# Linear attention before a mixture of experts: a product moved to GpSimd, and a scan's operand, small loads, bias and padding moved with it

## The chip, the cores and the metric

The kernel runs on one core of one Trainium2 chip. The metric is the device time of one execution in microseconds, as a median of repeated runs. The engines are named as the profile names them: PE (TensorE), DVE (VectorE), ACT (ScalarE), POOL (GpSimd) and SP, whose queue here only issues DMAs.

## What is computed

Three layers follow one another. The first is attention with a decaying state, for 4 batches, 8 heads, 768 tokens and heads of 48; the second sends each of the 3072 tokens through one of 8 experts, which a gate with a bias per modality chooses; the third is a dense layer with a squared relu.

```python
def _attn_ref(q, k, v, alpha):
    state = np.zeros((B, H, D, D), dtype=np.float32)
    for t in range(S):
        state = alpha[:, :, t, :, None] * state + np.einsum('bhd,bhe->bhde', k[:, :, t], v[:, :, t])
        y[:, :, t] = np.einsum('bhd,bhde->bhe', q[:, :, t], state)

def _moe_ref(x, modality_id, w_gate, modality_bias, w1, w2):
    logits = x @ w_gate + modality_bias[modality_id]
    e_idx = np.argmax(logits, axis=1)
    ...
    for e in range(E):
        mask = e_idx == e
        h = np.maximum(x[mask] @ w1[e], 0.0)
        out[mask] = gate_w[mask, None] * (h @ w2[e])

def _moe2_ref(x, w_in, w_out):
    r = np.maximum(x @ w_in, 0.0)
    return ((r * r) @ w_out).astype(np.float32)
```

## The kernel before

**Attention by chunks.** The 3072 tokens are 24 chunks of 128, six to a batch. In a chunk the decays are turned into running products, so that attention becomes matmuls. Queries, keys and decays of a chunk lie in one tile `qk` of 112 partitions: two heads side by side on rows 0 to 47 and 64 to 111, four pairs along the columns, with rows 48 to 63 as padding. For chunk n, `prep(n)` on DVE makes `acum`, the forward scan of the decays (line 472), its reciprocal at the chunk's end (473), `rs`, the backward scan (477), `qt`, the queries times `acum` (481), and `kt`, the keys times `rs` (483). A scan takes two operands, and the second here is `amin`, one constant column, spread over the row. It stands in column 384 of `kvc`, a PSUM bank, whose columns 0 to 383 PE writes with the products of keys and values. Engines do not touch one PSUM bank's tile at the same time in this kernel's trace: its `kvc` matmuls follow the scans, and the scans the matmuls.

**A round.** The loop runs over n from 0 to 23. PE does in order: `sp`, keys by queries of chunk n+1 (`qk_mm`, line 504); `kp`, the transpose of its `kt` (515); `kvc`, keys by values of chunk n (529); `y` of chunk n (554) and, from the second chunk of a batch on, its cross part with the state (557). ACT copies `sp` to `pm` (507), `kp` to `kT` (517) and `y` to `yt` (559). POOL masks `pm` of chunk n+1 (`affine_select`, 493; tied by hand to begin after the last operation of DVE that stands ahead of it) and multiplies the state by its decay (544). DVE does `prep(n+3)`, with two hooks: `kv_sd`, which adds the state (541, 543), between the two scans, and the jobs called "D", behind the backward scan. The code's order is the order of every engine's queue; nothing is reordered by a scheduler. A new `sp` needs `qt` and `kt`; a new `kvc` needs `kT` only, though the bank holds it for the scans as well.

**The gate.** Every fourth round `gate_lg` multiplies `yt` by the gate's weights into the bank `gps` (218); ACT copies it to `ls`, and `back` transposes it (226) into the same bank. In rounds 8 and 16 (eight chunks at a time) `gate_a` follows as a "D" job on DVE: `L`, `mx`, `dl` (238), `sc`, `sm`, `oh_all` (243). In the next round PE counts with `gate_b` (250, 252) from `oh_all`; DVE's `gate_s` makes the weights `gw` through `ss` (282 to 285) and `gate_c` the ranks. With `gw` ACT scales each chunk's transposed output (`xtr`, 293) to `xb` (297). From `bt_all`, `first_ids` picks, again into `gps`, the tokens of the first expert, which POOL gathers (633) near the end of the loop.

**The start.** SP's queue loads chunks 0 to 3 and three tiles of values, then the gate's weights `wg`, the modalities `mod`, the biases `mbias`, and writes zeros to a table `pbuf` in DRAM (194), then loads chunk 4 and so on. DMAs share eight counts in turn, so that each DMA waits for the one that last used its count; in the order's rows these counts are DMAHW0 to DMAHW7. `mask(0)` stands behind `qk_mm(0)`; the bias table `lbias` is made by five operations of DVE in round 2 (`setup_bias`).

**Behind attention** come the experts (three matmuls for one product in split precision) and the dense layer, whose conversions of weights run on POOL (lines 733 and 734).

Of the kernel before, what the change touches and what calls it, by code (L numbers as in the profile page):

```python
# [57 lines left out]
def body(ctx, tc, qka, v, alpha, mod, wg, mbias, w1, w2, w_in, w_out, out):  # L58
# [123 lines left out]
    def setup_gate():  # L182
# [11 lines left out]
        SY.dma_start(pbuf.rearrange("(o n) -> o n", n=C), sdt[2][:(NT + PAD) // C, :C].bitcast(I32))  # L194

    def setup_bias():
        modf = gc.tile([128, NTILE, 1], F32, name="modf")
        V.tensor_copy(modf, mod_sb[:, :, 0:1])
        modn = gc.tile([128, NTILE, 1], F32, name="modn")
        V.tensor_scalar(modn, modf, -1.0, 1.0, op0=ALU.mult, op1=ALU.add)  # L200
        lb1 = gc.tile([128, NTILE, NE], F32, name="lb1")
# [1119 lines left out]
```

## Time and profile before

| what | value |
|---|---|
| median of 3 runs | 776.43 us (776.18 to 777.32) |
| the profiled execution | 774.81 us, its span 773.0 us |
| granted PE clock, mean | 0.995 |
| busy share of the span | PE 96%, DVE 62%, ACT 42%, POOL 21% |

The page's busy shares are means over three layers of different kind. Attention lasts to about 124 us; experts and dense layer follow. To read a stretch, one takes the timeline of one engine at a time, finds two equal operations a round apart, and looks at the brackets, which give the idle time before an instruction and what ended it.

### The profile page before, as it was taken

The page shows a single profiled execution, that of the slowest core. Times are in us where ns is not written, and L with a number is a line of the kernel's source. Part 1 is how long each engine was busy: PE and PEld are TensorE (multiplying, and loading weights), DVE is VectorE, ACT ScalarE, POOL GpSimd, SP SyncE. Part 2 cuts the span into 40 slices and gives each one's busy share as a digit, 9 for nine tenths or more (in the row PEclk, how much of TensorE's full clock was granted, in tenths as well). Part 3 has the DMA queues.
Part 4 walks back from the last instruction along what each step waited for, and adds up shares of the span by engine and source line. Part 5 has one row for each costly group of instructions (what it writes and reads, how often), then busy time and mean ns, then how long its engine had stood idle before and what let it go on. Part 6 is the DMA issues. An engine that isn't in the chain of part 4 may idle for free.

```text
span 773.0 us, 13143 instructions
## 1 busy us (share of the span) xinstructions
PE 745.1 (96%) x5148; PEld 654.0 (85%) x5148; DVE 478.0 (62%) x812; ACT 323.8 (42%) x587; POOL 166.2 (21%) x185
## 2 busy tenths in 40 slices
PE   8898989999999999999999999999999999999994
PEld 6777778898788888889889989999899998999984
DVE  7999997877887867878744444544553333343340
ACT  3446467354444443546533323332332342333340
POOL 3332323234645454431100100010020001002001
PEclk9999999999999999999999999999999999999998
DMA  8988765579877886788300220040010000001001
GB/s 216 266 210 237 208 212 164 167 199 221 158 278 221 214 221 157 251 159 230 126 5 1 66 85 0 11 140 1 0 42 2 1 10 31 1 1 42 0 1 45
DMA packets 42814, 88.89 MB, mean 115 GB/s; under 512 B 11181, under 2 KB 26567, under 8 KB 42743
## 3 DMA queue, kind: packets, MB, share of 16 engines
q1 hardware_dynamic: 39543, 78.13, 36.1%
q0 software_dynamic: 3200, 9.83, 4.6%
q8 instruction: 42, 0.69, 0.4%
q14 instruction: 29, 0.24, 0.1%
HBM read 72.19 MB, written 15.76 MB: 114 GB/s over the span
## 4 chain that ended last, share of the span: by engine, by line
PE 76%; DVE 5%; DMA 2%; ACT 1%; issue 1%; POOL 0%; POOLq 0%; DVEq 0%; ACTq 0%
PE acc L660 8%; PE acc L658 8%; PE acc L659 8%; PE h L659 8%; PE h L660 8%; PE h L658 8%; PE hps L659 4%; PE hps L660 4%; PE oo L658 4%; PE oo L659 4%; PE oo L660 4%; PE hps L658 4%; DMA xg<-xs,ids 1%; DVE w2l L569 1%; PE xt L651 1%
## 5 line engine op out<-in xcount | busy, mean ns | idle before, releaser
L1044 DVE TENSOR_TENSOR r<-r 128x512 f32<-128x512 f32 x96 | 68.7, 716 | 143.8 <-ACT r L1043 143.7
L660 PE MATMUL acc<-w2h,hl 128*128 128x384 f32 x372 | 125.7, 338 | 0.3 <-DVE hl L569 0.2
L658 PE MATMUL acc<-w2h,hh 128*128 128x384 f32 x372 | 125.3, 337 | 0.6 <-ACT hh L568 0.6
L659 PE MATMUL acc<-w2l,hh 128*128 128x384 f32 x372 | 124.9, 336 | 0.0
L1043 ACT ACTIVATE r<-h 128x512 f32<-128x512 f32 x96 | 57.4, 598 | 154.4 <-PE h L660 153.0
L660 PE MATMUL h<-xh,w1l 128*128 128x512 f32 x288 | 113.8, 395 | 0.0
L659 PE MATMUL h<-xl,w1h 128*128 128x512 f32 x288 | 113.6, 395 | 0.0
L658 PE MATMUL h<-xh,w1h 128*128 128x512 f32 x288 | 112.1, 389 | 0.0
L569 DVE TENSOR_TENSOR hl<-r,hh 128x512 fp32r<-128x512 f32 x93 | 64.5, 694 | 63.9 <-PE acc L660 36.4
L1067 POOL DMA_INDIRECT out_dram<-ob,pidx x24 | 23.9, 995 | 366.4 <-ACT ob L1065 328.8
L568 ACT CAST hh<-r 128x512 fp32r<-128x512 f32 x93 | 57.7, 620 | 80.6 <-DVE r L1044 80.6
L658 PEld LDWEIGHTS acc<-w2h,hh 128*128 128x128 f32 x372 | 69.9, 188 | 5.1 <-ACT hh L568 1.0
L659 PEld LDWEIGHTS acc<-w2l,hh 128*128 128x128 f32 x372 | 69.8, 188 | 3.8
L660 PEld LDWEIGHTS acc<-w2h,hl 128*128 128x128 f32 x372 | 69.8, 188 | 1.0 <-DVE hl L569 1.0
L658 PE MATMUL oo<-hh,w2h 128*128 128x512 f32 (+1 forms) x192 | 68.7, 358 | 0.0
L658 PE MATMUL hps<-xh,w1h 128*128 128x512 f32 (+1 forms) x192 | 68.1, 355 | 0.0
L659 PE MATMUL hps<-xl,w1h 128*128 128x512 f32 (+1 forms) x192 | 67.4, 351 | 0.7 <-DVE xl L569 0.7
L660 PE MATMUL oo<-hh,w2l 128*128 128x512 f32 (+1 forms) x192 | 67.3, 350 | 0.0
L659 PE MATMUL oo<-hl,w2h 128*128 128x512 f32 (+1 forms) x192 | 67.2, 350 | 0.0
L660 PE MATMUL hps<-xh,w1l 128*128 128x512 f32 (+1 forms) x192 | 67.1, 350 | 0.0
L660 PEld LDWEIGHTS h<-xh,w1l 128*128 128x128 f32 x288 | 54.0, 188 | 11.5
L659 PEld LDWEIGHTS h<-xl,w1h 128*128 128x128 f32 x288 | 54.0, 187 | 9.2
(217 smaller groups left out, 1281.0 us busy)
## 6 DMA issues: line engine op xcount, KB each, us to landing
qk<-qka_dram SPq DMA_DIRECT2D x21, 679.0 KB, 5.7
raw<-w_dram SPq DMA_DIRECT2D x21, 512.0 KB, 8.1
raw<-w_dram SPq DMA_DIRECT2D x28, 384.0 KB, 4.2
cvr<-w_in_dram SPq DMA_DIRECT2D x12, 512.0 KB, 5.9
cvr<-w_out_dram SPq DMA_DIRECT2D x12, 512.0 KB, 11.6
vv<-v_dram SPq DMA_DIRECT2D x24, 192.0 KB, 6.7
xs<-xb SPq DMA_DIRECT2D x24, 192.0 KB, 3.5
alr<-alpha_dram SPq DMA_DIRECT2D x9, 512.0 KB, 3.4
```

Of the source, the lines that this page charges most:

```text
L568: A.copy(hi, raw)
L569: V.tensor_sub(lo, raw, hi)
L651: PE.transpose(xt[:, hf * 128:(hf + 1) * 128], xgs[i][:, hf, k * 128:(k + 1) * 128], ident)
L658: PE.matmul(o, ah, bh, start=start, stop=False)
L659: PE.matmul(o, ah, bl, start=False, stop=False)
L660: PE.matmul(o, al, bh, start=False, stop=stop)
L1043: A.activation(r, o, AF.Relu)
L1044: V.tensor_mul(r, r, r)
L1067: G.indirect_dma_start(out=out, out_offset=bass.IndirectOffsetOnAxis(ap=pidx[:, n:n + 1], axis=0), in_=ob, in_offset=None)
```

## The change

`kt` is made by POOL from chunk 2 on, in `prep` right behind the backward scan. `qt` is made ahead of the backward scan, between `kv_sd` and it, and the state's decay, still on POOL, is called behind `qt` and tied to begin after it. The "D" jobs stand behind `kt`. `amin` goes from `kvc` to column 511 of `gps`; the logits of `gate_lg` go from `gps` to a part of the current `y` tile. The four `qk` tiles are allocated once, and from chunk 4 on a chunk is loaded by two DMAs of 48 rows, without the padding rows. The loads of `wg`, `mod` and `mbias` and the write of `pbuf` go from SP's queue to ACT's. `setup_bias` is done by POOL, at the start behind `mask(0)`, and `mask(0)` stands behind `prep(1)`, tied to its last operation.

```diff
+        if n < 4:
+            qks.append(ld.tile([RP, 2 * NP * C + NP * CA], F32, name=f"qk{n}", bufs=1))
+        qk = qks[n % 4]
...
         else:
-            SY.dma_start(qk, qka[b, c])
+            for j in range(2):
+                SY.dma_start(qk[64 * j:64 * j + D], qka[b, c, 64 * j:64 * j + D])
...
-    amin = kvc[:, 2 * NP * D:2 * NP * D + 1]
+    gps = ps_g.tile([128, 512], F32, name="gps")
+    amin = gps[:RP, 511:512]
...
-        SY.dma_start(wg_sb[64 * j:64 * j + D, :, :NE], wg.rearrange("(p j d) e -> j d p e", j=2, d=D)[j])
+        A.dma_start(wg_sb[64 * j:64 * j + D, :, :NE], wg.rearrange("(p j d) e -> j d p e", j=2, d=D)[j])
...
-        SY.dma_start(pbuf.rearrange("(o n) -> o n", n=C), sdt[2][:(NT + PAD) // C, :C].bitcast(I32))
+        A.dma_start(pbuf.rearrange("(o n) -> o n", n=C), sdt[2][:(NT + PAD) // C, :C].bitcast(I32))
...
-        lt = gps[:, :128]
+        lt = gps[:, :128] if n_y[0] is None else n_y[0][:, 0, 2 * C:3 * C]
...
+        qt = xp.tile([RP, NP, C], F32, tag="xl", name="qt", bufs=4)
+        if n > 1:
+            V.tensor_mul(qt, qq, acum[:, :, 1:C + 1])
+        for f in mids[1:2]:
+            f(last_dve())
         rs = at2.tile([RP, NP, CA], F32, tag="rs", name="rs", bufs=1)
         V.tensor_tensor_scan(rs.rearrange("p a c -> p (a c)")[:, ::-1], al[:, ::-1], amin, AMIN, op0=ALU.mult, op1=ALU.max)
-        for f in mids[1:]:
+        kt = xp.tile([RP, NP, C], F32, tag="xh", name="kt", bufs=4)
+        if n < 2:
+            V.tensor_mul(qt, qq, acum[:, :, 1:C + 1])
+        (V if n < 2 else G).tensor_tensor(kt, kk, rs[:, :, 2:C + 2], op=ALU.mult)
+        for f in mids[2:]:
             f()
-        qt = xp.tile([RP, NP, C], F32, tag="xl", name="qt", bufs=4)
-        V.tensor_mul(qt, qq, acum[:, :, 1:C + 1])
-        kt = xp.tile([RP, NP, C], F32, tag="xh", name="kt", bufs=4)
-        V.tensor_tensor(kt, kk, rs[:, :, 2:C + 2], op=ALU.mult)
...
-    mask(0)
     k_T(0)
     warm(FILL)
     preps[1] = prep(1)
+    mask(0, last_dve())
+    setup_bias()
...
-    at(2, "mid", setup_bias)
...
-            preps[n + 3] = prep(n + 3, lambda: kv_sd(n), lambda: do(n, "D"))
+            preps[n + 3] = prep(n + 3, lambda: kv_sd(n), lambda i: decay(n, i), lambda: do(n, "D"))
```

In the order of ACT at its start, before, the conversions of six small tables are followed by the first copy of `pm`. The names in brackets are counts that an instruction waits for: PE_49 is PE's, Pool_49 POOL's, DMAHWn_49 a DMA's.

```order
L160 CAST tokid<-tokid_i 128x24 [waits Pool_49]
L160 CAST hidx<-hidx_i 128x22 [waits Pool_49]
L160 CAST slj<-slj_i 128x6 [waits Pool_49]
L160 CAST edesc<-edesc_i 128x8 [waits Pool_49]
L160 CAST eidx<-eidx_i 128x8 [waits Pool_49]
L507 COPY pm<-sp 128x512 [waits PE_49] x2
L517 COPY kT<-kp 128x448 [waits PE_49]
```

The same place now, with the DMAs that came from SP's queue:

```order
L151 DMA wg_sb<-wg_dram 48x4x8 [waits DMAHW0_49,Pool_49]
L151 DMA wg_sb<-wg_dram 48x4x8 [waits DMAHW1_49]
L153 DMA mod_sb<-mod_dram 128x48 [waits DMAHW2_49]
L155 DMA mb_sb<-mbias_dram 128x16 [waits DMAHW4_49]
L165 CAST rev<-rev_i 128x128 [waits Pool_49]
L165 CAST tokid<-tokid_i 128x24 [waits Pool_49]
L165 CAST hidx<-hidx_i 128x22 [waits Pool_49]
L165 CAST slj<-slj_i 128x6 [waits Pool_49]
L165 CAST edesc<-edesc_i 128x8 [waits Pool_49]
L165 CAST eidx<-eidx_i 128x8 [waits Pool_49]
L199 DMA pbuf<-sd_128 26x128 [waits DMAHW7_49]
L521 COPY pm<-sp 128x512 [waits PE_49] x2
```

The write of `pbuf` stands ahead of the first copy and waits for DMAHW7; the last DMA in SP's queue on that count at this point is the load of chunk 3.

In the order of DVE in round 8, with the gate's jobs ("D") of the first eight chunks, before:

```order
L472 SCALAR_TENSOR_TENSOR acum<-qk,kvc 112x528 [waits DMAHW4_49,PE_49]
L473 RECIPROCAL qk<-acum 112x4 [waits DVE_49]
L543 TENSOR_TENSOR sd_127<-kvc,sd_126 112x192 [waits Pool_49]
L477 SCALAR_TENSOR_TENSOR rs<-qk,kvc 112x528 [waits DVE_49]
L234 TENSOR_TENSOR L<-gps,lbias 128x64 [waits PE_49]
L236 TENSOR_REDUCE mx<-L 128x8 [waits DVE_49]
L238 TENSOR_TENSOR dl<-L,mx 128x64 [waits DVE_49]
L240 SCALAR_TENSOR_TENSOR sc<-dl,edesc 128x64 [waits DVE_49]
L242 TENSOR_REDUCE sm<-sc 128x8 [waits DVE_49]
L243 TENSOR_TENSOR oh_all<-sc,sm 128x64 [waits DVE_49]
L481 TENSOR_TENSOR qt<-qk,acum 112x512
L483 TENSOR_TENSOR kt<-qk,rs 112x512
```

The same round now:

```order
L478 SCALAR_TENSOR_TENSOR acum<-qk_110,gps 112x528 [waits DMAHW4_49,DMAHW3_49,PE_49]
L479 RECIPROCAL qk_110<-acum 112x4 [waits DVE_49]
L557 TENSOR_TENSOR sd_128<-kvc,sd_127 112x192 [waits Pool_49]
L484 TENSOR_TENSOR qt<-qk_110,acum 112x512
L488 SCALAR_TENSOR_TENSOR rs<-qk_110,gps 112x528 [waits DVE_49,Pool_49]
L240 TENSOR_TENSOR L<-gps,lbias 128x64
L242 TENSOR_REDUCE mx<-L 128x8 [waits DVE_49]
L244 TENSOR_TENSOR dl<-L,mx 128x64 [waits DVE_49]
L246 SCALAR_TENSOR_TENSOR sc<-dl,edesc 128x64 [waits DVE_49,Activation_49]
L248 TENSOR_REDUCE sm<-sc 128x8 [waits DVE_49]
L249 TENSOR_TENSOR oh_all<-sc,sm 128x64 [waits DVE_49]
L478 SCALAR_TENSOR_TENSOR acum<-qk_99,gps 112x528 [waits DMAHW7_49,DMAHW6_49,PE_49]
```

`qt` has moved ahead of the backward scan, `kt` is gone, and the forward scan waits for the transposed logits (PE_49) where it waited for `kvc` before; the backward scan waits for POOL, which reads the one `rs` buffer.

In the order of POOL at the end of attention, before, from the decay of round 20 on:

```order
L544 TENSOR_TENSOR sd_127<-sd_127,acum 112x192 [waits DVE_49]
L493 AFFINE_SELECT pm<-pm 128x512 [waits Activation_49] x2
L544 TENSOR_TENSOR sd_125<-sd_125,acum 112x192 [waits DVE_49]
L633 DMA xg<-xs,ids_e 128x384 [waits DMAHW4_49,DMAHW5_49,DMAHW3_49,DMAHW6_49,DMAHW2_49,DMAHW7_49,DMAHW1_49,DMAHW0_49]
L633 DMA xg<-xs,ids_e 128x384
L493 AFFINE_SELECT pm<-pm 128x512 [waits Activation_49] x2
L544 TENSOR_TENSOR sd_126<-sd_126,acum 112x192 [waits DVE_49]
```

The same stretch now:

```order
L492 TENSOR_TENSOR kt<-qk_107,rs 112x512 [waits DMAHW5_49,DMAHW4_49,DVE_49]
L508 AFFINE_SELECT pm<-pm 128x512 [waits Activation_49] x2
L563 TENSOR_TENSOR sd_128<-sd_128,acum 112x192 [waits DVE_49]
L492 TENSOR_TENSOR kt<-qk_110,rs 112x512 [waits DMAHW1_49,DMAHW0_49,DVE_49]
L508 AFFINE_SELECT pm<-pm 128x512 [waits Activation_49] x2
L563 TENSOR_TENSOR sd_126<-sd_126,acum 112x192 [waits DVE_49]
L652 DMA xg<-xs,ids_e 128x384 [waits DMAHW4_49,DMAHW3_49,DMAHW5_49,DMAHW2_49,DMAHW7_49,DMAHW1_49,DMAHW0_49]
L652 DMA xg<-xs,ids_e 128x384
L508 AFFINE_SELECT pm<-pm 128x512 [waits Activation_49] x2
L563 TENSOR_TENSOR sd_127<-sd_127,acum 112x192 [waits DVE_49]
```

A `kt` stands ahead of the masks and decays of its round, and that of chunk 23 ahead of the last two masks and the gathers.

## Rows read from the trace of the kernel before

**Rows 1.** The page's chain that ended last, by engine, as shares of the span.

```profile
PE 76%; DVE 5%; DMA 2%; ACT 1%; issue 1%; POOL 0%; POOLq 0%; DVEq 0%; ACTq 0%
```

**Rows 2.** Timeline of DVE: start us, us, engine, line, operation, out<-in, count [idle before].

```profile
42.09 1.25 DVE L472 TENSOR_TENSOR_SCAN acum<-qk,kvc 112x528 f32<-112x528 f32 x1
...
43.71 1.24 DVE L477 TENSOR_TENSOR_SCAN rs<-qk,kvc 112x528 f32<-112x528 f32 x1
44.87 0.66 DVE L481 TENSOR_TENSOR qt<-qk,acum 112x512 f32<-112x512 f32 x1
...
46.05 1.24 DVE L472 TENSOR_TENSOR_SCAN acum<-qk,kvc 112x528 f32<-112x528 f32 x1
```

**Rows 3.** Timeline of PE over the same round.

```profile
42.52 1.16 PE L504 MATMUL sp<-qt,kt 48*128 48x128 f32 x16
...
45.00 0.61 PE L529 MATMUL kvc<-vv,kT 128*64 128x48 f32 x15 [0.79 <-DVE rs L477]
...
47.08 1.16 PE L504 MATMUL sp<-qt,kt 48*128 48x128 f32 x16
```

**Rows 4.** Waits from 16 to 122 us: who for whom, us in total, times, longest.

```profile
PE kvc L529 <- DVE rs L477: 4.1, 6, 1.1
```

**Rows 5.** Timeline of the end of attention, all engines.

```profile
117.16 0.52 POOL L544 TENSOR_TENSOR sd<-sd,acum 112x192 f32<-112x192 f32 x1
...
117.20 0.53 DVE L238 TENSOR_TENSOR dl<-L,mx 128x32 f32<-128x32 f32 x1
...
120.57 0.48 DVE L283 TENSOR_SCALAR ss<-ss 128x4 f32<-128x4 f32 x1
...
121.02 1.23 POOL L493 TENSOR_SCALAR_AFFINE_SELECT pm<-pm 128x512 f32<-128x512 f32 x2
...
122.11 1.28 PE L554 MATMUL y<-pm,vv 128*48 128x128 f32 x16 [0.22 <-issue]
```

**Rows 6.** Timeline of the start of attention, all engines.

```profile
9.46 1.07 ACT L507 COPY pm<-sp 128x512 f32<-128x512 f32 x2 [5.49 <-PE sp L504]
...
10.12 1.67 POOL L493 TENSOR_SCALAR_AFFINE_SELECT pm<-pm 128x512 f32<-128x512 f32 x2 [6.29 <-ACT pm L507]
10.23 1.07 DVE L481 TENSOR_TENSOR qt<-qk,acum 112x512 f32<-112x512 f32 x1
...
12.77 0.41 SPq L194 DMA_DIRECT2D pbuf<-sd  x1
...
15.68 1.73 SPq L111 DMA_DIRECT2D qk<-qka_dram  x2
...
16.54 1.16 PE L504 MATMUL sp<-qt,kt 48*128 48x128 f32 x16
```

**Rows 7.** Timeline of two gate rounds and the round after, all engines.

```profile
50.31 0.33 PE L226 MATMUL gps<-ident,ls 128*128 128x128 f32 x1
...
50.43 1.25 DVE L472 TENSOR_TENSOR_SCAN acum<-qk,kvc 112x528 f32<-112x528 f32 x1 [0.33 <-PE kvc L529]
...
53.71 0.22 DVE L238 TENSOR_TENSOR dl<-L,mx 128x64 f32<-128x64 f32 x1
...
54.76 0.19 PE L250 MATMUL gps<-oh_all,lt_b 128*128 128x72 bf16 x1 [0.28 <-DVE oh_all L243]
...
59.34 0.73 ACT L297 ACTIVATE xb<-xtr,gw 128x192 f32<-128x192 f32 x2 [0.34 <-DVE R L261]
...
92.48 0.19 PE L250 MATMUL gps<-oh_all,lt_b 128*128 128x72 bf16 x1 [0.93 <-DVE oh_all L243]
```

**Rows 8.** Instructions of lines 733 and 734: durations in ns (least/median/most), first and last start.

```profile
L733 POOL TENSOR_TENSOR cvr<-cvr,cvt x24: 1298/1319/2177, 168.1 to 371.9; 128x512 f32<-128x512 f32 x24
...
L734 POOL TENSOR_TENSOR cvt<-cvr x24: 1040/1636/1906, 170.4 to 374.1; 128x512 f32<-128x512 f32 x24
```

**Rows 9.** Windows at the end: length, busy PE PEld DVE ACT POOL, PEclk, DMA, GB/s.

```profile
763.00:764.00 1.00, 0.25 (x2) 0.00 (x0) 0.00 (x0) 0.48 (x1) 0.00 (x0) 1.00 0.02 8
...
765.50:766.00 0.50, 0.00 (x0) 0.00 (x0) 0.00 (x0) 0.00 (x0) 0.23 (x1) 0.50 0.00 0
```

More of the change, by code (lines that the diff above doesn't have):

```diff
@@ L193, in setup_gate @@
         G.memset(oh_all, 0.0)
-        SY.dma_start(pbuf.rearrange("(o n) -> o n", n=C), sdt[2][:(NT + PAD) // C, :C].bitcast(I32))
+        A.dma_start(pbuf.rearrange("(o n) -> o n", n=C), sdt[2][:(NT + PAD) // C, :C].bitcast(I32))
     def setup_bias():
         modf = gc.tile([128, NTILE, 1], F32, name="modf")
-        V.tensor_copy(modf, mod_sb[:, :, 0:1])
+        G.tensor_copy(modf, mod_sb[:, :, 0:1])
         modn = gc.tile([128, NTILE, 1], F32, name="modn")
-        V.tensor_scalar(modn, modf, -1.0, 1.0, op0=ALU.mult, op1=ALU.add)
+        G.tensor_scalar(modn, modf, -1.0, 1.0, op0=ALU.mult, op1=ALU.add)
         lb1 = gc.tile([128, NTILE, NE], F32, name="lb1")
         shp = [128, NTILE, NE]
-        V.tensor_tensor(lbias, mb_sb[:, 0:1, :].to_broadcast(shp), modn.to_broadcast(shp), op=ALU.mult)
-        V.tensor_tensor(lb1, mb_sb[:, 1:2, :].to_broadcast(shp), modf.to_broadcast(shp), op=ALU.mult)
-        V.tensor_add(lbias, lbias, lb1)
+        G.tensor_tensor(lbias, mb_sb[:, 0:1, :].to_broadcast(shp), modn.to_broadcast(shp), op=ALU.mult)
+        G.tensor_tensor(lb1, mb_sb[:, 1:2, :].to_broadcast(shp), modf.to_broadcast(shp), op=ALU.mult)
+        G.tensor_add(lbias, lbias, lb1)
     def over(t, sh):
@@ L475, in prep, with beside @@
             f()
+        qt = xp.tile([RP, NP, C], F32, tag="xl", name="qt", bufs=4)
[3 more added lines that the diff above has]
+            f(last_dve())
         rs = at2.tile([RP, NP, CA], F32, tag="rs", name="rs", bufs=1)
         V.tensor_tensor_scan(rs.rearrange("p a c -> p (a c)")[:, ::-1], al[:, ::-1], amin, AMIN, op0=ALU.mult, op1=ALU.max)
-        for f in mids[1:]:
-            f()
-        qt = xp.tile([RP, NP, C], F32, tag="xl", name="qt", bufs=4)
-        V.tensor_mul(qt, qq, acum[:, :, 1:C + 1])
-        kt = xp.tile([RP, NP, C], F32, tag="xh", name="kt", bufs=4)
-        V.tensor_tensor(kt, kk, rs[:, :, 2:C + 2], op=ALU.mult)
+        kt = xp.tile([RP, NP, C], F32, tag="xh", name="kt", bufs=4)
[3 more added lines that the diff above has]
+        for f in mids[2:]:
+            f()
         ae = acum[:, :, C:C + 1]
         return dict(ae=ae, qt=qt, kt=kt)
-    preps, pms, kTs, kvs, sds, xts, yts = {}, {}, {}, {}, {}, {}, {}
+    preps, pms, kTs, kvs, sds, xts, yts, decays = {}, {}, {}, {}, {}, {}, {}, {}
     def last_dve():
         return next(i for i in reversed(nc.cur_bb.bb.instructions) if i.engine == ET.DVE)
+    def beside(i, after):
+        if after is not None:
+            tc.add_manual_dep(i.ins, after.name, mybir.DependencyInfo(mybir.DependencyClass.Sync, mybir.DependencyReason.DATA), reason="beside the scans")
     def mask(n, after=None):
@@ L493, in mask @@
             m = G.affine_select(out=pm, in_=pm, pattern=[[0, 4], [1, C]], compare_op=ALU.is_ge, fill=0.0, base=0, channel_multiplier=-1)
-            if after is not None:
-                tc.add_manual_dep(m.ins, after.name, mybir.DependencyInfo(mybir.DependencyClass.Sync, mybir.DependencyReason.DATA), reason="beside the scans")
-                after = None
+            beside(m, after)
+            after = None
     def qk_mm(n):
@@ L543, in kv_sd, with decay @@
         V.tensor_add(sv, kv, sds[n][:, :NP * D].rearrange("r (p d) -> r p d", d=D))
-        G.tensor_tensor(sv, sv, ae, op=ALU.mult)
+        decays[n] = sv, ae
+    def decay(n, after=None):
+        if n in decays:
+            sv, ae = decays.pop(n)
+            beside(G.tensor_tensor(sv, sv, ae, op=ALU.mult), after)
     def y_mm(n):
         vv, pm, pr = vs.pop(n), pms.pop(n), preps[n]
-        y = ps_a.tile([128, 2, 512], F32, tag="y", name="y")
+        y = n_y[0] = ps_a.tile([128, 2, 512], F32, tag="y", name="y")
         cross = n % NCH > 0
@@ L830, in body @@
         if n + 3 < N:
-            preps[n + 3] = prep(n + 3, lambda: kv_sd(n), lambda: do(n, "D"))
+            preps[n + 3] = prep(n + 3, lambda: kv_sd(n), lambda i: decay(n, i), lambda: do(n, "D"))
         else:
             kv_sd(n)
+            decay(n)
             do(n, "D")
@@ L849, in body @@
     actx.close()
+    n_y[0] = None
     ps_y = pool(gctx, "ps_y", space=PSUM, side="right")
```

11 lines of the change are left out of this document (6 added, 5 removed).

## The prediction

> **What bounds the kernel now.** I read the chain that ended last first, then one plain round of attention on DVE and on PE, then the waits of the attention phase. The chain [rows 1] is PE's for 76%: the experts and the dense layer behind attention run one matmul after another, so whatever moves the end of attention moves the end of the program by the same amount. Everything below is therefore a shift of attention's end.
>
> In a plain round DVE goes from one forward scan to the next in 46.05 − 42.09 = 3.96 us [rows 2], without a gap. PE takes 47.08 − 42.52 = 4.56 [rows 3], of which 0.79 is a wait, so its own work is 3.77. That wait is the reader's first find: PE's `kvc` matmuls start at 45.00, when the backward scan of 43.71 (1.24 long) ends. They share no data with it; the scan's second operand `amin` lies in the same PSUM bank. From 16 to 122 us this wait is seen six times, 4.1 in all [rows 4]. DVE and PE are thus almost level, and POOL has room: a mask of 1.23 and a decay of 0.52 a round [rows 5].
>
> **Start of attention: +5.4 (0 to 7).** The order of ACT puts the write of `pbuf` ahead of the first copy of `pm`, and makes it wait for DMAHW7. That count belongs to the load of chunk 3. Before, the write went from SP at 12.77 on another count, and SP's next load, which waits for DMAHW7, left at 15.68 though nothing else held it [rows 6]: chunk 3 lands then. So ACT, which had idled 5.49 and copied at 9.46, stands until 15.7, takes 0.4 to issue (as SP's 0.41), and copies from 16.1; two copies take 1.07, so the second chunk's `sp` starts at 17.2. The other three small loads fall in ACT's 5.49 of idleness, at no cost; without that cover they are 0.4 each. Behind the copy stand, on POOL, the first mask (16.7, 1.23 long), then the bias: three operations of 192 columns at the decay's 0.52 and two of 24 columns, at 0.2 like the 64 columns of `dl` [rows 7]: 2.0, to 19.9. Only then comes the first `kt` on POOL.
>
> The price of that `kt` is not in the trace. The nearest rows are POOL's products and sums of 128x512 in the dense phase [rows 8]: 1.30 at least and 1.32 in the median for the product, 1.04 at least for the sum, up to 1.9 for the sum and 2.2 for the product beside other work. I take 1.25, near the product because `kt` is one. The Trainium skill, page GPSIMD Engine Reference, section 3.1, gives 4497 ns for an fp32 sum of 2048 columns, an estimate of 1.12 for 512; the sum rows reach below that and the product rows stand above it, so the measured product decides; by 1.12 the whole sum would be some 0.7 lower.
>
> A second price is DVE and POOL hindering each other. Beside a mask of 1.67 (1.23 at other times) the two products of DVE at 10.23 and after it take 1.07 each instead of 0.66 [rows 2, 6]; beside a decay a `dl` of 32 columns takes 0.53, and one with twice the columns, alone, 0.22 [rows 5, 7]. So `kt` on POOL stretches or waits where DVE runs an operation with two SBUF inputs, here `qt` of the next chunk: up to 0.6. With it `kt` ends at 19.9 + 1.25 + 0.6 = 21.8, and `sp` of chunk 2 starts at about 22.0 against 16.54: +5.4. The low end, 0, is a wait that is met before ACT gets there; the high end, 7, is `kt` at its 1.9 plus a late load.
>
> **Recovery in plain rounds: −4.1 (−4.1 to −3).** Without `kt`, whose share is half of the 46.05 − 44.87 = 1.18 of both products, DVE's round is 3.96 − 0.59 = 3.37, at most 0.35 longer where POOL hinders it. PE's own 3.77 then bounds. So the gain is not 0.59 for each of twenty rounds: it is what PE waits now, 4.1 [rows 4], since the scans no longer lie in `kvc`'s bank.
>
> **The two gate rounds (8 and 16): +3.4 (1.7 to 3.4).** Now `amin` lies in the bank into which `back` transposes the logits, and the order gives the forward scan a wait for PE there; queued behind it on DVE are `qt`, the backward scan and the whole gate, and PE waits for `oh_all` at its `gate_b`. Before, from `back` to `gate_b` pass 54.76 − 50.31 = 4.45, and PE is already waiting at the end of it: 0.28, in the second gate 0.93 [rows 7]. So each delay passes on. Three come: the scan starts after `back` (50.31 + 0.33 + 0.05) instead of at 50.43, +0.26; `qt` stands ahead of the backward scan, +0.59; `dl`, two SBUF inputs, is reached 0.4 after the backward scan while `kt` is in its 1.25 on POOL, +0.85 if it is held to the end as in rows 5. Together 1.7, twice. The low end leaves the last one out.
>
> **The rounds after them (9 and 17): +2.1 (0 to 2.1).** ACT's `xb` waits for the weights `gw` (at 59.34, idle 0.34 before it [rows 7]). `kt`'s 0.59 is gone from DVE and `qt`'s 0.59 is put ahead of the backward scan: no difference. But the sum `ss` follows 0.2 behind that scan, where `kt` starts on POOL; even four columns of it took 0.48 beside POOL's work at the end [rows 5]. Held to the end of `kt` that is 1.25 − 0.2 = 1.05, twice.
>
> **End of attention: +1.9 (0 to 2.4).** There POOL's order is the whole queue: `kt` of chunk 23 now stands ahead of mask 22, decay 21, the two gathers and mask 23. Mask 23 starts at 121.02 as soon as the gathers are issued, and PE's last `y` follows at 122.11 [rows 5]. A queue of one after the other is 1.25 longer; I add 0.65 for a POOL held up while DVE does the expert split, and the last scan's wait for the matmuls of the first ids, in the same bank. Zero would be a gather that is issued no later, since it waits for its ids anyway.
>
> **What I cost at nothing.** The logits in `y`'s bank: `y` stands behind `back` on PE, and `back` already needs the copy that reads them. The padding rows and second DMA a chunk: a load is issued in round n and scanned in round n+2, so that one round less of lead is covered; the `qk` buffers now come free when POOL has read them, a `kt` later. If that cover were gone a scan would wait, as at the start. The decay behind `qt`: its reader, the cross part of the next `y`, comes a round later.
>
> **The sum.** 5.4 − 4.1 + 3.4 + 2.1 + 1.9 = +8.7, on the profiled execution's 774.81: 783.5. The median of the runs is 1.62 above that execution (776.43), so the forecast is 785.1, put as 785.0. The ends of the terms give −2.4 and +11.9; few of them come together, and I take 782 to 789 as this case's own range.
>
> **Rivals.** (a) POOL does not hinder DVE, because `kt` ends beside the next scan: the start loses 0.6, the gate rounds 1.7, the next rounds 2.1: +4.3, 780.7. (b) ACT is not held, or chunk 3 lands early: 5.4 falls away: +3.3, 779.7. (c) The other side: DVE's shorter round builds a lead. Neither the hold on ACT nor `kt` reaches PE; besides the 4.1, the 0.28 + 0.93 at the gates goes; the queue at the end costs its 1.25: −4.0, 772.4. It decides from the point where the write of `pbuf` leaves before ACT's first copy is due and the forward scan is a round ahead of `back`. For it speaks DVE's round of 3.37 against PE's 3.77; against it the wait for DMAHW7 and the row at 15.68. (d) No visible effect, gain and loss about equal: 776.4. (e) POOL becomes the bound: `kt` at 1.9 as the slowest sum [rows 8], a mask of 1.23, a decay of 0.52 and two waits of some 0.25 make 4.1 against PE's 3.77; 20 rounds at 0.35 more: 783.5 + 7 + 1.6 = 792.
>
> A last one belongs to the clock. PE's last matmul ends in the slice from 763 to 764 us, whose granted clock is 1.00; some two us later the clock is 0.50, its lower level of 1.2 GHz [rows 9]. With ACT held PE has nothing from its fill matmuls to 17.2. The Trainium skill, page TensorE: Matmul & The Clock Gate, Part 1, says that the throttled state is the default and that activity releases it; the rows on the idle end agree, and no row shows attention's start after such a pause. If the first round ran at half clock its 3.77 would be 7.54, to 24.7 instead of 22.0: +2.7 at most, 787.8, inside the range; it is part of the first case, and I count it at nothing, since the pause may not come at all.
>
> **Chances.** Forecast 0.60; (a) 0.10; (b) 0.08; (c) 0.11; (d) 0.05; (e) 0.06. The range of 776 to 789 takes in the forecast's own, (a), (b) and (d), leaving out (c), (e) and the edges. A measurement of this kernel can tell 0.2%, or 1.55 us, from no change: faster 0.11, same 0.07 ((d) and the near edges of (b) and (c)), slower 0.82.
>
> **What would show it.** In the changed kernel: ACT's first `pm` copy at about 16 us and not at 10, `sp` of chunk 2 at 22 (the start); no wait of PE's `kvc` for a scan (the recovery); `back` to `gate_b` 6.1 instead of 4.45; `kt` on POOL at 1.25 alone, and `dl` and `ss` beside it stretched; the last `y` waiting for POOL about 2 us later than attention's other shift. A first copy at 10 us, or `dl` at 0.22 right behind the backward scan, would make me wrong in the direction of (b), (a) or (c); `kt` over 1.8 in plain rounds, in that of (e).

## The result, and the profile after

The changed kernel takes 781.32 us in the median of five runs (780.11 to 783.74), the kernel before 776.43 (775.02 to 777.32): a ratio of 1.0067, with a 95% interval of 1.0048 to 1.0086. It is slower by about 5 us, in the direction of the forecast of 785.0 and inside the range of 776 to 789 that its chances take in, but 0.7 under the 782 to 789 that it called this case's own range. By the time alone rival (a), 780.7, lies nearer than the forecast; which of them is right is told by the rows. The profiled execution took 780.11, its span 778.2.

Where the 5.2 us between the two profiled spans (773.0 and 778.2) arise is read by following one instruction of PE through the rounds, the `sp` of each chunk, which is the first of its round:

| `sp` of chunk | before, us | after, us | after minus before | stretch that ends here |
|---|---|---|---|---|
| 2 | 16.54 | 20.89 | +4.35 | start |
| 10 | 52.19 | 52.77 | +0.58 | plain rounds: −3.77 |
| 11 | 56.68 | 60.16 | +3.48 | first gate: +2.90 |
| 12 | 62.27 | 65.35 | +3.08 | round after: −0.40 |
| 18 | 89.85 | 92.93 | +3.08 | plain rounds: 0 |
| 19 | 94.93 | 100.97 | +6.04 | second gate: +2.96 |
| 20 | 101.41 | 106.61 | +5.20 | round after: −0.84 |
| 23 | 117.77 | 122.97 | +5.20 | 0 |
| first expert matmul | 125.55 | 131.91 | +6.36 | end of attention: +1.16 |
| last matmul of PE | 762.91 | 770.03 | +7.12 | experts: +0.76 |
| end of the span | 773.0 | 778.2 | +5.2 | behind the last write: −1.9 |

**The start.** The timeline of the changed kernel, all engines (columns as in [rows 2]); line 199 is the write of `pbuf`, 521 the copy of `pm`, 518 `sp`, 208 the bias, 492 `kt`:

```profile
13.62 0.61 ACTq L199 DMA_DIRECT2D pbuf<-sd  x1
14.27 1.07 ACT L521 COPY pm<-sp 128x512 f32<-128x512 f32 x2 [4.37 <-DMA qk<-qka_dram]
...
14.91 2.36 PE L518 MATMUL sp<-qt,kt 48*128 48x128 f32 x16 [3.24 <-ACT pm L521]
...
16.69 0.52 POOL L208 TENSOR_TENSOR lbias<-mb_sb,modn 128x192 f32<-128x192 f32 x1
...
18.30 1.09 POOL L492 TENSOR_TENSOR kt<-qk,rs 112x512 f32<-112x512 f32 x1
...
20.89 1.89 PE L518 MATMUL sp<-qt,kt 48*128 48x128 f32 x16
```

The write leaves at 13.62, and only then comes ACT's first copy, at 14.27 instead of 9.46 [rows 6]. `sp` of chunk 1 waits 3.24 for it and then takes 2.36 instead of 1.16; on POOL the bias and `kt` follow the mask, and `sp` of chunk 2 starts at 20.89. The reason for the 2.36 is in the windows of PE (length, busy time, granted clock, DMA share, GB/s):

```profile
15.00:16.00 1.00, 1.00 (x9) 0.82 0.72 118
16.00:17.00 1.00, 1.00 (x11) 0.50 1.18 197
...
22.00:23.00 1.00, 1.00 (x13) 0.77 1.05 186
```

From 11.7 to 14.9 us PE has nothing; from about 15.6 the clock is 0.50, the level of 1.2 GHz, and goes back to 1.00 in the slice from 22 to 23. The kernel before has 1.00 in every slice here. PE does not wait for `kt`, which ends at 19.39: it gets through its own round at half clock only at 20.89, and `sp` of chunk 2 follows without idle time.

**A gate round**, same columns; line 232 is `back`, 478 the forward scan, 244 `dl`, 256 `gate_b`, 573 `y`, 289 `ss`:

```profile
50.89 0.33 PE L232 MATMUL gps<-ident,ls 128*128 128x128 f32 x1
...
51.26 1.25 DVE L478 TENSOR_TENSOR_SCAN acum<-qk,gps 112x528 f32<-112x528 f32 x1 [1.58 <-PE gps L232]
...
54.81 1.10 POOL L492 TENSOR_TENSOR kt<-qk,rs 112x512 f32<-112x512 f32 x1 [0.64 <-DVE rs L488]
...
55.14 0.85 DVE L244 TENSOR_TENSOR dl<-L,mx 128x64 f32<-128x64 f32 x1
...
56.89 0.22 PE L256 MATMUL gps<-oh_all,lt_b 128*128 128x72 bf16 x1 [1.83 <-DVE oh_all L249]
...
57.30 1.98 PE L573 MATMUL y<-pm,vv 128*48 128x128 f32 x16
...
61.03 1.06 DVE L289 TENSOR_SCALAR ss<-ss 128x8 f32<-128x8 f32 x1
```

The scan waits for `back` (idle 1.58), `dl` is held for 0.85 while `kt` is on POOL, PE waits 1.83 for `oh_all` where it waited 0.28 [rows 7], and the `y` behind that wait takes 1.98 instead of 1.09, at half clock. Before, the `y` of that round, and `ss` in it:

```profile
55.06 1.09 PE L554 MATMUL y<-pm,vv 128*48 128x128 f32 x16
...
58.84 0.17 DVE L283 TENSOR_SCALAR ss<-ss 128x8 f32<-128x8 f32 x1
```

And the windows of PE now:

```profile
57.00:58.00 1.00, 1.00 (x16) 0.50 1.07 206
...
60.00:61.00 1.00, 1.00 (x22) 0.99 1.00 205
```

In the second gate the wait is 2.35 and `y` takes 1.76. PE's waits for `kvc` [rows 4] have no row any more in the list of waits from 16 to 130 us; this one stands in their place:

```profile
PE gps L256 <- DVE oh_all L249: 4.2, 2, 2.4
```

### The profile page after: what moved, and what is told of

Its sections match the earlier page's. It is cut to its first block, busy times and chain, and to the rows that moved or that the text cites. A ratio compares the mean times of both kernels' runs of the same rounds, so it can differ in the third digit from the quotient of the medians.

```text
span 778.2 us, 13199 instructions
## 1 busy us (share of the span) xinstructions
PE 750.4 (96%) x5148; PEld 658.5 (85%) x5148; DVE 472.2 (61%) x785; ACT 323.5 (42%) x587; POOL 193.9 (25%) x212
## 4 chain that ended last, share of the span: by engine, by line
PE 71%; DVE 6%; DMA 4%; issue 1%; ACT 1%; POOL 1%; SPq 0%; POOLq 0%; DVEq 0%; ACTq 0%
PE acc L679 8%; PE acc L677 8%; PE acc L678 8%; PE h L678 8%; PE h L679 8%; PE h L677 8%; PE oo L677 3%; PE oo L678 3%; PE oo L679 3%; PE hps L678 3%; PE hps L679 3%; PE hps L677 3%; DMA raw<-w_dram 2%; DMA xg<-xs,ids 1%; DVE w2l L588 1%
## 5 line engine op out<-in xcount | busy, mean ns | idle before, releaser
L752 POOL TENSOR_TENSOR cvr<-cvr,cvt 128x512 f32<-128x512 f32 x24 | 33.9, 1412 | 112.9 <-ACT hh L984 25.7
```

Of the source, the lines that this page charges most:

```text
L752: G.tensor_tensor(lf, lf, f, op=ALU.mult)
```

## Experiments

Two theories stood against each other. The first: the cost is the start (ACT held by the write) and the scans' bank in the gate rounds, each with a stretch at half clock behind it, while `kt` on POOL is a gain. The rival: `kt` on POOL is the cost, since POOL and DVE hold each other up. Ratios are to the kernel before, with 95% intervals.

**The write alone back on SP.**

```diff
-        A.dma_start(pbuf.rearrange("(o n) -> o n", n=C), sdt[2][:(NT + PAD) // C, :C].bitcast(I32))
+        SY.dma_start(pbuf.rearrange("(o n) -> o n", n=C), sdt[2][:(NT + PAD) // C, :C].bitcast(I32))
```

> The changed kernel, with only the write of pbuf back in SP's queue; the other small loads stay on ACT. First theory (the hold on ACT at the start, and the half clock that follows it, are one of the costs): the first pm copy is at about 10 us instead of 14.3, no slice near 16 to 22 us has a granted clock of 0.50, sp of chunk 2 starts at 16.5 to 17.5 instead of 20.9, and the time falls by 3.4 to 4.4, to 777 to 778. Rival (kt on POOL, which holds up DVE, is the cost; the start is made good later anyway): sp of chunk 2 may come earlier, but the end does not: at most 1 lower, 780.3 or more.

Measured: 789.54, a ratio of 1.0160 (1.0112 to 1.0208). The first theory missed, and the rival did not foresee it either. The first copy is at 9.79 and `sp` of chunk 2 at 17.99 instead of 20.89 (the theory had 16.5 to 17.5; PE waits 3.2 for `kt`, which stands behind the bias), the half clock comes later, from 20.0 to 23.5, and the kernel is slower than the changed one. The timeline of PE in that run:

```profile
43.55 0.74 PE L543 MATMUL kvc<-vv,kT 128*64 128x48 f32 x15 [2.67 <-issue]
```

And windows of PE there (columns as above):

```profile
40.00:48.00 8.00, 5.33 (x63) 0.79 1.04 202
...
44.00:46.00 2.00, 2.00 (x23) 0.50 1.04 192
```

PE stands 2.67 ahead of the `kvc` of chunk 6, for something the profile doesn't name, and runs the next matmuls at half clock. From 40 to 48 us the DMA engines are busy at 1.04 and move 202 GB/s; a later group of runs is about that.

**`amin` back in `kvc`'s bank, all else as changed.**

```diff
-    amin = gps[:RP, 511:512]
+    amin = kvc[:, 2 * NP * D:2 * NP * D + 1]
```

> The changed kernel, with only amin back in kvc's bank; kt stays on POOL, the logits stay in y's bank. First theory (in the gate rounds the scan's wait for the transposed logits costs PE a wait and then a stretch at half clock): PE's waits for oh_all, 1.83 and 2.35, fall below 1 each, no half clock after 57 and 97 us, 2.9 less at each gate, some waits of kvc come back: 775 to 777. Rival (kt on POOL, beside which dl and ss are held, is the cost): the gate's dl still takes 0.85, the waits for oh_all stay over 1.3, and the time falls by at most 1.5, to 779.8 or more.

Measured: 785.70, 1.0102 (1.0062 to 1.0142). The first theory missed: the bank alone does not undo the gate's cost. The timeline of that run, DVE and PE at the first gate and behind it:

```profile
56.66 0.84 DVE L244 TENSOR_TENSOR dl<-L,mx 128x64 f32<-128x64 f32 x1
...
58.41 0.19 PE L256 MATMUL gps<-oh_all,lt_b 128*128 128x72 bf16 x1 [1.44 <-DVE oh_all L249]
...
61.90 1.05 DVE L289 TENSOR_SCALAR ss<-ss 128x8 f32<-128x8 f32 x1
...
64.07 0.84 PE L299 MATMUL xtr<-ident,yt 112*128 112x112 f32 x4 [1.44 <-ACT xb L303]
```

And windows of PE there (columns as above):

```profile
58.00:60.00 2.00, 1.59 (x34) 1.00 0.97 223
...
64.00:66.00 2.00, 1.93 (x16) 0.57 0.26 98
```

The wait at `gate_b` falls from 1.83 to 1.44 only, since `qt` and the held `dl` are still ahead of it; the clock stays up there, but the next round's `xtr` waits 1.44 for `xb`, whose `gw` was held by `kt` (`ss` took 1.05), and there the half clock begins. The rival's signs all came: `dl` at 0.84, waits over 1.3 (1.44, and 2.10 at the second gate), a time over 779.8. So `kt` beside the gate's jobs is part of the cost; that it is all of it does not follow.

**`kt` back on DVE, in its new place.**

```diff
-        (V if n < 2 else G).tensor_tensor(kt, kk, rs[:, :, 2:C + 2], op=ALU.mult)
+        V.tensor_tensor(kt, kk, rs[:, :, 2:C + 2], op=ALU.mult)
```

> The changed kernel, with only kt back on DVE, in its new place right behind the backward scan and ahead of the gate's jobs. First theory: dl falls from 0.85 to 0.22 and ss from 1.06 to 0.17, but kt's 0.6 now stands ahead of them on DVE, so the wait for oh_all stays; DVE's plain round goes back to about 3.96, over PE's 3.7: 781 to 785. Rival (POOL's hindering of DVE is the cost): 777 to 778.

Measured: 788.35, 1.0135 (1.0090 to 1.0180); slower than either theory said. With `kt` off POOL, `dl` is back at 0.23 and `ss` at 0.17, so it was POOL's `kt` that held them; but now `kt` itself stands ahead of them on DVE, and the wait is 2.10. The rival's 777 to 778 is far off, but as one delay replaces the other here, this run does not price the hold. Part of the slowness lies at the end of the span, 2.4 us longer behind the last write than in the changed kernel (below). The timeline of DVE and PE in that run:

```profile
56.49 0.69 DVE L492 TENSOR_TENSOR kt<-qk,rs 112x512 f32<-112x512 f32 x1
...
57.61 0.23 DVE L244 TENSOR_TENSOR dl<-L,mx 128x64 f32<-128x64 f32 x1
...
58.73 0.19 PE L256 MATMUL gps<-oh_all,lt_b 128*128 128x72 bf16 x1 [2.10 <-DVE oh_all L249]
```

**PE's pauses filled with matmuls that nobody reads.**

```diff
-WARM, FILL = 8, 5
+WARM, FILL = 8, 13
...
+                if g < 2:
+                    at(n + 1, "B", lambda: warm(4))
```

> The changed kernel with idle time of PE filled by matmuls whose result nobody reads: 8 more behind the first k_T, 4 more ahead of gate_b in rounds 9 and 17. Nothing else changes, and no wait of the others goes. First theory (the stretches at half clock are a cost of their own): the granted clock stays at 1.00 at 16 to 22, 57 to 60 and 97 to 101 us, y there takes 1.09 instead of 1.98 and 1.76, and the time falls by 2 to 4, to 777 to 779. Rival (the half clock lies beside waits that are there anyway): the clock stays up but the time moves by less than 1.

Measured: 783.89, 1.0104 (1.0053 to 1.0155); missed. At the start the fill does what it should: the clock is 1.00 from 12 to 24 us. But `sp` of chunk 2 gains only 0.36 (20.53), since it waits 1.34 for `kt` on POOL, and behind the first gate the clock is down at 58 to 62 us all the same. There the fill did not fall into the pause: PE stood ahead of the last two `kvc`, and the fill came behind them, at 57.01:

```profile
56.83 0.25 PE L543 MATMUL kvc<-vv,kT 128*48 128x48 f32 x2 [1.86 <-issue]
```

At the second gate `y` took 1.09, and the clock fell behind the next wait, of 2.31 at `xtr`.

**Are the loads late?** The four runs above kept the change's split loads. What they share in their slow places is a DMA rate of some 190 GB/s at engines that are busy all the time, where the kernel before moves 240 to 263. So the loads were changed alone, on both kernels, and the changed kernel was run again beside them.

```diff
         else:
-            for j in range(2):
-                SY.dma_start(qk[64 * j:64 * j + D], qka[b, c, 64 * j:64 * j + D])
+            SY.dma_start(qk, qka[b, c])
```

> The changed kernel, with the chunks from the fifth on loaded whole by one DMA of 112 rows, as before the change, into the same four tiles. New theory (two DMAs of 48 rows without the padding move bytes more slowly than one of 112 with it: at engines busy for 1.03 to 1.05 the changed kernel moved 183 to 202 GB/s from 16 to 56 us, the kernel before 240 to 263): the rate goes back to 240 or more in 24 to 48 us; the time changes by little, since in the changed kernel the start holds PE back and the loads keep up: 779 to 781, the spread of runs narrower. Rival (the rate is low because POOL and DVE are busy beside the DMAs, or because of the order of the queue): the rate stays near 190 and the time where it is, within 1 of the changed kernel's.

The reverse edit, on the kernel before:

> The kernel before, with only its loads changed: four qk tiles allocated once, and from the fifth chunk on two DMAs of 48 rows. New theory: the rate falls from 240 to 263 to under 210 GB/s in 24 to 48 us, the forward scans wait for loads, and the time rises by 2 to 6, to 779 to 783. Rival (the loads are not the cause): 775.5 to 778, rate over 230.

Both undone, the split and the write on ACT:

> The changed kernel, with whole loads and the write of pbuf on SP's queue: both suspects of the start and of the loads undone, the scans' bank and kt on POOL kept. New theory (with the write on SP alone PE started earlier and ran into the late loads, which is why that run was slower): start at 16.5 to 18 for sp of chunk 2, no wait for loads from 36 to 62 us, gates still at a wait of about 2 with half clock: 777 to 780, at least 6 below the run with the write on SP alone. Rival (something else of the earlier start, not the loads, made that run slow): 785 or more.

The changed kernel itself:

> The changed kernel itself, on the chip of these runs, as the measure for the others. Both theories: 780 to 783.7 as before; if it lies at 784 or more on this chip, the times of the earlier four have to be compared with it and not with 781.3.

Measured: the changed kernel 783.96, 1.0060 (1.0039 to 1.0081), as in its first runs by ratio; whole loads 782.45, 1.0060 (1.0037 to 1.0083); the kernel before with split loads 780.08, 1.0018 (0.9999 to 1.0037); whole loads and the write on SP 784.11, 1.0065 (1.0041 to 1.0089). Windows from 40 to 48 and 48 to 56 us (length, PE busy, clock, DMA share, GB/s), of the changed kernel, of whole loads, and of the kernel before with split loads:

```profile
40.00:48.00 8.00, 7.75 (x143) 1.00 1.01 183
48.00:56.00 8.00, 7.06 (x137) 1.00 1.05 186
```

```profile
40.00:48.00 8.00, 7.76 (x135) 1.00 0.69 192
48.00:56.00 8.00, 8.00 (x152) 1.00 0.98 259
```

```profile
40.00:48.00 8.00, 6.93 (x138) 1.00 1.00 202
48.00:56.00 8.00, 7.72 (x152) 1.00 0.92 176
```

By share of busy time the changed kernel moves 183 / 1.01 = 181 GB/s and 186 / 1.05 = 177, whole loads 192 / 0.69 = 278 and 259 / 0.98 = 264, split loads in the kernel before 202 and 191. Earlier the gap is smaller: from 16 to 40 us, by eights, split loads in the kernel before have 218, 225 and 231 (under 210 was expected from 24 on), the kernel before itself 264, 258 and 250. All bytes moved are counted here, not those of the chunks alone. So two DMAs of 48 rows move bytes more slowly than one of 112 rows with the padding, by a margin that varies. In the changed kernel it costs nothing that is seen (1.0060 with and without), perhaps because the late start gives the loads time; its 779 to 781 were missed all the same. In the kernel before it costs little, 1.4 us by the ratio, under the 2 to 6 that were expected and not clear of noise. With the early start it costs 7: 1.0160 against 1.0065, the one difference being the loads. That is what made the first run slow, though no row shows by which wait, and it clouds the other three of its group: their loads were split, so they are used here only for the rows shown, not for their times.

The early start did not show in the time even so: 1.0065 against 1.0060, and the 777 to 780 that were expected were missed. What was next in line is in the timeline of that run's start (lines 202 and 491 are the first step of the bias and `kt`, 517 is `sp`):

```profile
15.51 0.20 POOL L202 CAST modf<-mod_sb 128x24 f32<-128x24 int32 x1 [2.47 <-DMA mod_sb<-mod_dram]
...
18.18 1.09 POOL L491 TENSOR_TENSOR kt<-qk,rs 112x512 f32<-112x512 f32 x1
...
19.33 2.08 PE L517 MATMUL sp<-qt,kt 48*128 48x128 f32 x16 [4.33 <-POOL kt L491]
```

The bias on POOL waits for `mod`, whose load lands at 15.5; `kt` of chunk 2 stands behind it, PE waits 4.33, and the clock falls again. One hold stood behind the other.

**The start undone**: whole loads, the write on SP, and

```diff
     mask(0, last_dve())
-    setup_bias()
...
+    at(2, "mid", setup_bias)
```

with the five operations on DVE again.

> The changed kernel with all that concerns its start undone except the three small loads on ACT: the write of pbuf on SP, whole loads, and the bias made by DVE in round 2 again instead of by POOL ahead of the first kt. The scans' bank and kt on POOL stay. Theory (three things hold the start, one behind the other: the write on ACT, the bias on POOL behind its load, and the half clock after PE's pause): sp of chunk 2 at 16.5 to 17.5, clock 1.00 from 12 to 25 us, 3 to 4.5 lower than the run with the bias still on POOL: a ratio to the kernel before of 1.001 to 1.003. Rival (what is gained at the start is lost again in the gate rounds, where PE waits for DVE anyway): 1.005 or more.

Measured: 781.59, 1.0041 (1.0019 to 1.0064). `sp` of chunk 2 starts at 15.82 and the clock is 1.00 throughout, as the theory says; the gain of 3.5 at that place over the run before is down to 1.65 at chunk 10 (50.89 against 52.54). A forward scan now waits for its load, and in round 4 `back` waits 1.19 for a backward scan that stands behind the bias on DVE. From the list of that run's waits, 12 to 130 us (who for whom, us in total, times, longest):

```profile
DVE acum L477 <- DMA qk<-qka_dram: 2.6, 1, 2.6
```

The time lies between theory and rival. At the gate nothing has changed: a wait of 1.82, `y` at 1.98. The profiled execution, 778.22, is one of the shorter of twelve (777.56 to 784.84), and their length goes with the mean granted clock: the four at 0.993 or 0.994 took 777.6 to 779.7, the five at 0.984 to 0.986 took 782.6 to 784.8. Its rows are thus those of an execution with little half clock.

**The gates, too.** In the seven rounds where the gate's matmuls write `gps`, the scans read `amin` from `kvc`; in five of them `qt` and `kt` are made by DVE behind the gate's jobs. Elsewhere `kt` stays on POOL. The fifth, round 20, makes the `kt` of chunk 23, so the queue at the end of attention is undone with it.

```diff
+    IN_KVC, LATE = (4, 8, 9, 12, 16, 17, 20), (8, 9, 16, 17, 20)
     def prep(n, *mids):
+        amin = amins[n - 3 in IN_KVC]
+        late = n - 3 in LATE
...
-        (V if n < 2 else G).tensor_tensor(kt, kk, rs[:, :, 2:C + 2], op=ALU.mult)
+        (V if n < 2 or late else G).tensor_tensor(kt, kk, rs[:, :, 2:C + 2], op=ALU.mult)
```

> The run above, and in the rounds where the gate's matmuls write their bank (4, 8, 9, 12, 16, 17, 20) the scans take amin from a second column in kvc's bank; in rounds 8, 9, 16, 17 and 20 qt and kt are made by DVE behind the gate's jobs, as before the change. In all other rounds kt stays on POOL. Theory (bank in the gate rounds, and kt ahead of the gate's jobs, are the second cost): no wait of PE for oh_all over 1, no half clock at the gates, 5 to 7 lower than the run above: a ratio of 0.993 to 0.997, faster than both kernels. Rival (POOL and DVE hinder each other in plain rounds too, and that is the cost): 1.000 or more.

Measured: 775.04, 0.9963 (0.9944 to 0.9983): faster than the kernel before by 0.37%, and 0.78% or 6 us below the run above, as expected. Bank and `kt` were switched together here, so this run does not tell their shares. From `sp` of chunk 23 to the first expert matmul pass 7.78 as in the kernel before, in the run above 9.18. The first gate's wait is 0.36 and no half clock follows. In round 17 one does; PE's timeline there:

```profile
95.78 0.60 PE L299 MATMUL xtr<-ident,yt 112*128 112x112 f32 x4 [1.62 <-ACT xb L303]
```

And a window of PE there (columns as above):

```profile
98.00:99.00 1.00, 1.00 (x9) 0.50 0.89 315
```

`xtr` waits 1.62 for `xb`, as long as the longest such wait of the kernel before (1.6, at a clock of 1.00), and here the clock falls behind it. `sp` of chunk 19 is 1.93 ahead of the kernel before, that of chunk 20 only 0.49. How much of the 0.37% is won in attention at all is in question: in the profiled executions PE's last matmul comes 0.65 later than before (763.56), and the span is 1.5 shorter only because 6.1 us instead of 8.2 lie behind the last write (764.77 before, 765.41 here).

**The fill, on the clean base.** The run with the start undone, and `warm(4)` ahead of `gate_b`:

> The run with the start undone, and four matmuls that nobody reads ahead of gate_b in rounds 9 and 17, in PE's idle time; no wait goes. Theory (the half clock behind a gate's wait is a cost of its own, beside the wait): clock 1.00 at the gates, y there 1.09 instead of about 1.9, 1.3 lower at each gate: 2 to 2.7 lower than without the fill. Rival (what follows waits for DVE anyway): less than 0.7 lower.

Measured: 781.03, 1.0038 (1.0022 to 1.0054): no faster than without. PE's timeline:

```profile
52.04 1.99 PE L141 MATMUL warm<-wrm 112*128 112x256 f32 x8
...
54.25 1.09 PE L572 MATMUL y<-pm,vv 128*48 128x128 f32 x16
...
60.14 1.01 PE L298 MATMUL xtr<-ident,yt 112*128 112x112 f32 x4 [1.99 <-ACT xb L302]
61.08 1.98 PE L572 MATMUL y<-pm,vv 128*48 128x128 f32 x16
```

At the gate it looks as the theory says: the clock stays at 1.00, `y` takes 1.09, and from `sp` of chunk 10 to that of chunk 11 pass 6.05 instead of 7.42. Then PE comes to `xtr` earlier, waits 1.99 there for the `gw` that `kt` held, and runs that round at half clock instead. From chunk 10 to 12 it takes 14.22, without the fill 12.58.

But the same came without any fill, in the profile of the changed kernel's second run (the measure of the loads' group):

```profile
56.87 0.19 PE L256 MATMUL gps<-oh_all,lt_b 128*128 128x72 bf16 x1 [1.83 <-DVE oh_all L249]
...
57.18 1.09 PE L573 MATMUL y<-pm,vv 128*48 128x128 f32 x16
...
63.07 1.01 PE L299 MATMUL xtr<-ident,yt 112*128 112x112 f32 x4 [1.99 <-ACT xb L303]
64.01 1.98 PE L573 MATMUL y<-pm,vv 128*48 128x128 f32 x16
```

The wait at `gate_b` is 1.83 as in its first profile, yet the clock stays at 1.00 behind it and falls only at `xtr`; from chunk 10 to 12 it takes 14.23. In the other five profiles with this wait and no fill the clock falls there. So behind the same pause it fell in one execution and not in the other, and one profile with the fill does not show what the fill did. What stands is the time: filling the pause alone gains nothing, as DVE is late all the same and the half clock comes at one pause or the next. That the half clock is free does not follow (the twelve runs above).

**The bank alone, on the kernel before**: the logits in `y`'s bank and the same switch of `amin`, `qt` and `kt` on DVE in their old places.

> The kernel before, with only the bank changed: logits in y's bank, the scans' amin in gps in the plain rounds and in kvc in the rounds where the gate writes gps. kt and qt stay on DVE in their old places. Theory (the scans' bank gave PE the wait of 4.1 in all; without kt on POOL DVE's round of 3.96 takes its place as the bound over PE's 3.7): 0 to 2 lower than the kernel before, a ratio of 0.997 to 1.000, and at least 2 slower than the switched kernel above. Rival (the bank alone is the gain and kt on POOL brings nothing): as fast as the switched kernel within 1.

Measured: 777.24, 0.9995 (0.9973 to 1.0017), 2.2 us slower than the switched kernel by medians. The bank brings nothing by itself, as DVE's round takes the place of the wait: `sp` of chunks 8 and 9 start 3.96 apart (42.30 and 46.26), in the switched kernel 3.70. `kt` on POOL is what makes room in plain rounds: `sp` of chunk 18 is 1.9 ahead of the kernel before in the switched kernel, 0.4 here. But in the profiles that lead is gone again by chunk 20, behind the half clock of round 17, and of the 2.2 us some 2.0 lie behind the last write (6.1 against 8.1). So the rival's number is missed, but the time does not show what `kt` gives in attention.

## The prediction, step by step

**Direction and size.** Slower was right; of the +8.6 forecast, 4.9 were measured. The steps, against the table above, which is one execution's:

- **Start, +5.4; measured +4.35.** The links up to `kt` held: the write ahead of the copy, the bias and `kt` behind it. The last did not: `kt` ended at 19.39, 2.4 sooner than forecast, and PE was not waiting for it but still in its own round at half clock, which had been counted at nothing (`sp` 2.36 instead of 1.16, 5.98 from `sp` of chunk 1 to that of chunk 2). That the sum came near is partly luck: the load landed 2 us sooner, 13.6 instead of 15.7 (in other runs with the write on ACT the write left as late as 15.14), and the half clock took some of it back. Undoing the hold alone, with whole loads, moved nothing in the time; the bias stood behind it.
- **Recovery, −4.1; measured −3.77.** Right: the waits at `kvc` are gone.
- **Gate rounds, +3.4; measured +5.86.** From `back` to `gate_b` 56.89 − 50.89 = 6.00 was measured, 6.1 forecast. What the step missed is what PE does behind the longer wait: `y` and its cross part at half clock, 0.89 and 0.37 more in the first gate. The clock had been priced at the start only. In the second profile of the same kernel the first gate costs 1.56, near the 1.7 forecast, and the round after it 2.59, with the half clock there.
- **Rounds after, +2.1; measured −1.24.** The hold of `ss` is there (1.06 instead of 0.17), but PE, late from the half clock, reaches `xtr` hardly before it, so it is mostly hidden; the fill run and the second profile of the changed kernel show it uncovered, with a wait of 1.99 each. The two gate terms together were 5.5 forecast and 4.62 measured.
- **End of attention, +1.9; measured +1.16**, by the queue that was named; the switched kernel, with chunk 23's `kt` back on DVE and the bank switched in that round, has none of it. The timeline of the changed kernel there:

```profile
121.31 1.10 POOL L492 TENSOR_TENSOR kt<-qk,rs 112x512 f32<-112x512 f32 x1 [0.64 <-DVE ids_e L340]
...
126.67 1.23 POOL L508 TENSOR_SCALAR_AFFINE_SELECT pm<-pm 128x512 f32<-128x512 f32 x2
...
128.19 1.09 PE L573 MATMUL y<-pm,vv 128*48 128x128 f32 x16 [0.19 <-issue]
```

`kt` stands ahead of mask 22; the last mask starts at 126.67 and PE's last `y` at 128.19, 6.08 later than before [rows 5], where its `sp` was 5.20 later.
- **The shift is rigid: not quite.** PE's last matmul is 7.1 later, the end of the span 5.2. Behind the last write's issue the span lasts 5.9 (772.26 to 778.2) instead of 8.2 (764.77 to 773.0), and with `kt` back on DVE, by one line, 8.3 (777.88 to 786.2). In that order:

```profile
772.26 0.97 POOL L1088 DMA_INDIRECT out_dram<-ob,pidx  x1 [3.68 <-DMA out_dram<-ob,pidx]
```

```profile
764.77 0.97 POOL L1067 DMA_INDIRECT out_dram<-ob,pidx  x1 [3.31 <-DMA out_dram<-ob,pidx]
```

```profile
777.88 0.97 POOL L1088 DMA_INDIRECT out_dram<-ob,pidx  x1 [3.25 <-DMA out_dram<-ob,pidx]
```

In all fourteen profiles it goes by `kt`: 5.9 to 6.2 in the ten runs that make it on POOL, at least in plain rounds, 8.1 to 8.5 in the four that make all of it on DVE. So the move of `kt` shortens the end by about 2.2, by a mechanism that no row shows. That is where more than half of the gap between forecast and result arises, and the sum had no term for it.

**The price of `kt`** was 1.25; it takes 1.09. Here the Trainium skill (GPSIMD Engine Reference, section 3.1), set aside for the rows of the dense phase, would have been nearer with its estimate of 1.12; by it the sum would have been 0.7 lower. **Hindering**: `dl` 0.85 instead of 0.22 and `ss` 1.06 instead of 0.17, both ending with `kt`, and back at 0.23 and 0.17 in the run with `kt` on DVE. Taken at their bounds, and rightly, though the bounds were 0.85 and 1.05 more and 0.63 and 0.89 were measured; so rival (a), whose time is nearest, does not have the right mechanism. (One reading was slightly off: of the two products of DVE beside the mask at the start the second takes 1.11, not 1.07.) `ss` has a single input and is held too. The Trainium skill (SBUF — State Buffer, Who interferes with whom) counts `tensor_scalar` among the operations that can take the port pair shared with POOL; the trace agrees, with the 1.06.

**Costed at nothing**: the split loads. In the changed kernel that holds by the run with whole loads; with an early start it does not (1.0160 against 1.0065). So the cover may have been the late start rather than the round of lead that was named. **The rivals**: (b), no hold on ACT, would have been 3.3 slower than before instead of 8.7; undoing the hold brought nothing. (c), DVE's lead, shows in the switched kernel's plain rounds, but its −4.0 is not reached (0.9963), and about 2 us of what is lie behind the last write.

Open: by what the span behind the last write is 2.2 shorter with `kt` on POOL; why the clock falls behind one pause of PE and not behind another of the same length (1.62, and 1.83 in one and the same kernel); how the gate's cost divides between the bank and `kt`; and what the last three of the first four runs would take with whole loads.

## What to carry to other kernels

Here moving an operation to an engine with room paid in the plain rounds and cost in those where a chain of small operations stood beside it: such a move has to be weighed round by round, by what stands behind it on both queues. And a lead at one place is not yet time: look where it goes, to the very end of the span. A shared bank is a wait for whoever writes it; look for the rounds in which the new neighbour is the one on the path. A small DMA that is put on a compute engine's queue holds that queue for the count that it waits for, and when one such hold is taken away, the next in line decides.

## What was not expected of the hardware

With two DMAs of 48 partitions (291 KB each) for a chunk, the DMA engines moved 177 to 231 GB/s by their busy share in the stretches of 8 us from 16 to 56 us (the changed kernel, and the kernel before with split loads), with one of 112 partitions (679 KB) 238 to 278 (the kernel before, and the changed one with whole loads). Behind pauses of PE of 1.4 to 3.2 us came 3 to 10 us at 1.2 GHz, but not behind each: behind a wait of 1.83 the next two groups took 1.26 longer in one execution of the changed kernel and nothing longer in another, where the fall came at the next pause. The end of the span behind the last write was some 2.2 us shorter in every run that made `kt` on POOL, in the plain rounds at least.
